# Routed attention and a SiLU MLP on one core: one-hot codes turned by themselves, new engine choices and a new order of heads

## The chip, the cores and the metric

The kernel runs on one core of a Trainium2 chip. The time is the device time of one execution in microseconds (us); the median of three runs of the kernel before is 308.21 (307.46 to 309.07). Lower is better. The engines are named as in the profile: PE (TensorE, its weight loads are PEld), DVE (VectorE), ACT (ScalarE), POOL (GpSimd), SP (SyncE, which here only issues transfers).

## The reference, cut to what matters

```python
# attention: q, k, v are (4, 8, 768, 64), centroids (8, 16, 64)
q_n = q / (np.linalg.norm(q, axis=-1, keepdims=True) + 1e-06)
k_n = ...
c_n = ...
q_assign = np.argmax(np.einsum('bhsd,hcd->bhsc', q_n, c_n), axis=-1)
k_assign = np.argmax(np.einsum('bhsd,hcd->bhsc', k_n, c_n), axis=-1)
mask = q_assign[:, :, :, None] == k_assign[:, :, None, :]
scores = np.where(mask, scale * np.matmul(q, k.transpose(0, 1, 3, 2)), -1000000000.0)
attn = softmax(scores)
attn_out = np.matmul(attn, v)
# MLP: x is (3072, 512), w_in (512, 2048), w_out (2048, 512)
x = attn_out.transpose(0, 2, 1, 3).reshape(B * S, H * D)
h = x @ w_in
return (h * (1.0 / (1.0 + np.exp(-h)))) @ w_out
```

Each query and each key is given to the nearest of 16 centroids of its head; a query attends only to the keys of its own centroid. The result of all heads goes through an MLP. `softmax` stands for the max, exp, sum and division of the source.

## The kernel before

**Scheme.** Tokens lie in tiles of 128, six tiles for a sequence (NJ = 6), so that a head's q and k are 12 tiles of 128 x 64. Each is multiplied by 128 and split into a high and a low half in fp16 (`hi`, lines 527 to 531, and `lo`, line 535), which lie side by side in a tile of `hl`, 128 columns. That tile is turned, so that features lie on partitions: by TensorE through a PSUM bank (line 570, copied out by a "settle", lines 585 and 587, into `lt`), which batch 0 does, or by one turning transfer of 12 tiles from `hl` into `ab` (line 550, issued by SP), which the other three batches do. The turned tiles are multiplied with the split centroids `stk` (lines 615 and 619 where the two terms add in the bank, `twin`, else line 624). From these logits VectorE takes the best centroid (a reduction and a comparison), which gives a code of 16 columns for every token, a mark at the query's centroid or at all but the key's. The code stands beside the high half in the scores product (line 801): 64 rows of data and 16 of code, so that a query and a key of other centroids get a term of 16384 in size that takes the exponential to 0. The exponential is on ScalarE (line 808), 288 of 128 x 512; the product with V (line 829) has a column of ones that yields the sum; VectorE takes the reciprocal (842) and normalises (847) into `xn`, one `xn` for the two heads of a pair. `xn` is turned into `xt`, by TensorE and a copy (877, 882, 884) or by a transfer (866). The MLP runs by units of two or three token tiles: up (907), tanh on ScalarE (913), gate on VectorE (918), down (942), copied out by ScalarE or VectorE (955, 957) and stored by SP (960). With y = h/2, SiLU is y(1 + tanh(y)).

**Codes before.** In batch 0 the code is written beside the high half in `hl`, and high half and code, 80 columns, are turned a second time by TensorE, one tile at a time (line 570 again, 96 tiles in all). The copy out of the bank multiplies each partition by `gain`, 1 for the data and 16384 for the code (lines 581 and 583), into `ab`. In the later batches VectorE turns the codes in blocks of 32 x 32 (line 715), and four copies put the quarters of a tile's tokens into rows 64 to 79 of `ab`: three on GpSimd (line 732), one as a transfer of SP (line 728), for each of the 24 heads.

**Loops.** Work is cut into parts (`part`): in batch 0 a head or a pair of heads with its keys and its first two query tiles, then the other four query tiles; later one head with 12 tiles. Batch 0 goes in two rounds, `ROUNDS` (0,2) and (2,6): all eight heads with two query tiles, then all eight with four; each of the others goes by heads over six tiles. MLP units lie between heads, as they become ready and by the due times `ML`.

**What sets the order.** Every operation is a `step` with an engine, a planned duration, what it comes after, the buffers it uses and a due time (`key`). A planner (class `Plan`) runs through time, gives each free engine its most urgent ready step, and the instructions are then emitted in the planned order; each engine executes its own in that order, and semaphores hold the real dependences. Buffers come from rings of fixed counts (`nk` and `nq` hold loaded K and Q, `nv` the loaded V, `hl`, `ab`, `vt` V in fp16, `P` exponentials, `Df` and `oh` and `ohT` stages of the codes, and eight PSUM banks); a step that needs a ring's next buffer waits until its old content has been read. Loads of K, Q and V, turning transfers and stores are all issued by SP in planned order; weights by GpSimd, each behind a tiny `pace` copy (line 974). Where the planner sees TensorE idle early in the run, it puts in "unread" matmuls of zeros (line 353, 128 x 256), as long as planned time is below `UNREAD`, 80000 ns.

**Choices.** The lists of lines 305 to 323 say which engine does what: `VC` casts V (line 415 on ACT, 417 on POOL), `TK` and `TQ` the settles of batch 0's first round, `TR` and `TS` of its second, `HI` and `HR` its high splits, `PUTB` the four code copies of the later batches, `XT` and the last argument of `attention` how `xn` is turned, `EVAC` the copies of the MLP's output. `AT` holds the due times of the rounds, `LEADS` how far ahead of them parts are started.

**Centroids.** They are loaded first, squared and summed, and their norm is taken as a power of 0.5 on GpSimd (line 433); then they are divided, split, turned by TensorE and put into `stk` by four copies.

## Time and profile before

| | before |
|---|---|
| median of 3 runs | 308.21 us (307.46 to 309.07) |
| the profiled execution | 307.14 us |
| its span in the trace | 305.3 us |
| mean granted TensorE clock | 0.998 |
| first unread matmul / first real instruction on TensorE | 1.05 / 5.53 us |
| first scores / first MLP matmul / first tanh | 11.82 / 34.90 / 35.96 us |
| end of the last matmul | 301.65 us |
| exponentials (L808, ScalarE) | 288, 157.8 us |
| down (L942), up (L907), scores (L801), V product (L829) on TensorE | 97.1, 95.6, 90.9, 49.8 us busy |
| code copies on GpSimd (L732) | 72, 39.3 us |
| code copies as transfers of SP (L728) | 24 |
| casts of V on GpSimd (L417) | 26, 14.6 us |
| lower splits on VectorE (L535) | 62, 40.7 us |
| tanh (L913), gates (L918) | 144 and 144, 67.8 and 70.1 us |

How to read it: the span runs from the first to the last instruction of the profiled execution, and the execution's own time has about 1.8 us around it. Busy times of TensorE overlap (a matmul starts before the one before it has ended), so that they add to more than the span holds; what one instruction costs is the time between its start and the next one's. The idle time of an engine is put down to the one that released it. An instruction's form reads output <- inputs, partitions x elements and type, so that "bank<-ident,hl 128x128" is a turn of a 128-column tile of `hl` into a PSUM bank, and "ab<-hl" a turning transfer.

### The profile page before, as it was taken

What the parts mean: (1) busy time and instruction counts of PE and PEld (TensorE: products, weight loads), DVE (VectorE), ACT (ScalarE), POOL (GpSimd) and SP (SyncE); (2) the same over time, 40 slices, a digit from 0 to 9 for tenths busy, and PEclk for the clock granted to TensorE, in tenths of its full rate; (3) what the DMA queues carried; (4) which work ended last, traced back from release to release, by engine and by line L of the source; (5) the groups of instructions that cost most, each with busy time, mean ns of one, the idle gap of its engine ahead of it and who ended that gap; (6) DMA issues with size and microseconds to landing.
All of it is one profiled execution on the core that took longest, in us unless ns stands there. A gap on an engine that the chain in (4) does not pass through costs nothing.

```text
span 305.3 us, 8425 instructions
## 1 busy us (share of the span) xinstructions
PE 297.3 (97%) x3257; PEld 196.1 (64%) x3257; DVE 207.9 (68%) x493; ACT 223.7 (73%) x461; POOL 108.2 (35%) x218
## 2 busy tenths in 40 slices
PE   8999999999999999999999998999999999999995
PEld 6898777577677746666656765665655565554644
DVE  5999688778869955989766997867562323750820
ACT  5869999888988838999777998778782380642721
POOL 2546432656466480717564563733000000000000
PEclk9999999999999999999999999999999999999999
DMA  7999969993969888486969848472010201002001
GB/s 245 290 249 251 206 104 224 103 248 87 226 100 237 191 167 196 138 156 162 237 149 223 155 154 169 131 129 66 0 37 36 84 12 71 35 0 73 32 34 69
DMA packets 73688, 41.82 MB, mean 137 GB/s; under 512 B 53041, under 2 KB 70705, under 8 KB 73649
## 3 DMA queue, kind: packets, MB, share of 16 engines
q1 hardware_dynamic: 68944, 36.94, 51.4%
q0 software_dynamic: 4288, 4.20, 8.6%
q8 instruction: 25, 0.41, 0.6%
q10 hardware_dynamic: 416, 0.16, 0.2%
q14 instruction: 15, 0.11, 0.1%
HBM read 27.30 MB, written 6.29 MB: 110 GB/s over the span
## 4 chain that ended last, share of the span: by engine, by line
PE 80%; DMA 7%; ACT 5%; DVE 3%; issue 1%; POOL 1%; SPq 0%; ACTq 0%; POOLq 0%
PE bank L942 27%; PE bank L907 22%; PE bank L801 16%; PE bank L829 9%; ACT P L808 4%; DMA ab<-hl 3%; PE bank L570 3%; DMA wout_s<-in_moe_w_out_dram 2%; PE bank L624 2%; DMA nk<-in_k_dram 2%; POOL hl L531 1%; PE bank L615 1%; DVE hl L535 1%; DVE gq L918 1%; PE bank L619 1%
## 5 line engine op out<-in xcount | busy, mean ns | idle before, releaser
L808 ACT ACTIVATE P<-bank 128x512 f16<-128x512 f32 x288 | 157.8, 640 | 30.8 <-PE bank L801 29.1
L942 PE MATMUL bank<-wout_s,gq 128*128 128x512 f16 (+1 forms) x400 | 97.1, 370 | 0.4 <-DMA wout_s<-in_moe_w_out_dram 0.4
L907 PE MATMUL bank<-xt,win_s 128*128 128x384 f16 (+1 forms) x576 | 95.6, 308 | 0.0
L918 DVE SCALAR_TENSOR_TENSOR gq<-tn,bank 128x384 f16<-128x384 f32 (+1 forms) x144 | 70.1, 504 | 32.4 <-ACT tn L913 28.7
L801 PE MATMUL bank<-ab 80*128 80x256 f16 (+1 forms) x384 | 90.9, 326 | 0.0
L913 ACT ACTIVATE tn<-bank 128x384 f32<-128x384 f32 (+1 forms) x144 | 67.8, 488 | 24.1 <-PE bank L907 20.9
L907 PEld LDWEIGHTS <-win_s 128*128 128x128 f16 x576 | 55.0, 97 | 28.8
L942 PEld LDWEIGHTS <-gq 128*128 128x128 f16 x400 | 37.9, 98 | 33.1 <-issue 0.7
L829 PEld LDWEIGHTS <-P 128*128 128x128 f16 x1152 | 45.6, 97 | 11.9 <-ACT P L808 0.8
L829 PE MATMUL bank<-vt,P 128*128 128x65 f16 x1152 | 49.8, 193 | 0.7 <-ACT P L808 0.6
L732 POOL COPY ab<-ohT 16x384 f16<-16x384 f16 x72 | 39.3, 546 | 28.2 <-DVE ohT L715 11.7
L801 PEld LDWEIGHTS <-ab 80*128 80x128 f16 x384 | 34.6, 97 | 20.7 <-DVE ab L583 0.2
L673 POOL TENSOR_TENSOR Df<-L,mx 128x192 f32<-128x192 f32 x24 | 12.3, 511 | 41.9 <-DVE mx L661 39.7
L957 DVE COPY ot<-bank 128x512 f32<-128x512 f32 x18 | 12.3, 681 | 16.4 <-PE bank L942 15.6
L535 DVE SCALAR_TENSOR_TENSOR hl<-nk,hl 128x384 f16<-128x384 f32 (+1 forms) x29 | 19.8, 687 | 3.3 <-POOL hl L531 3.1
L535 DVE SCALAR_TENSOR_TENSOR hl<-nq,hl 128x384 f16<-128x384 f32 (+3 forms) x33 | 20.9, 635 | 0.6 <-POOL hl L531 0.3
L641 DVE TENSOR_REDUCE L<-bank 128x192 f32<-128x384 f32 x24 | 13.3, 552 | 10.0 <-PE bank L624 9.7
L847 DVE TENSOR_TENSOR xn<-bank,rz 128x384 f16<-128x384 f32 (+2 forms) x40 | 19.1, 477 | 1.4 <-DVE rz L842 0.2
L531 POOL TENSOR_SCALAR hl<-nk 128x384 f16<-128x384 f32 (+1 forms) x25 | 13.6, 547 | 7.6 <-PE bank L570 6.7
L955 ACT COPY ot<-bank 128x512 f32<-128x512 f32 (+1 forms) x7 | 3.7, 524 | 17.2 <-PE bank L942 17.2
L531 POOL TENSOR_SCALAR hl<-nq 128x384 f16<-128x384 f32 (+2 forms) x27 | 15.2, 566 | 1.7 <-DMA nq<-in_q_dram 1.1
L417 POOL CAST vt<-nv 128x384 f16<-128x384 f32 x26 | 14.6, 582 | 1.1 <-DMA nv<-in_v_dram 0.7
(60 smaller groups left out, 183.6 us busy)
## 6 DMA issues: line engine op xcount, KB each, us to landing
nv<-in_v_dram SPq DMA_DIRECT2D x16, 384.0 KB, 5.6
out_dram<-ot SPq DMA_DIRECT2D x23, 256.0 KB, 2.3
nk<-in_k_dram SPq DMA_DIRECT2D x15, 384.0 KB, 4.3
nq<-in_q_dram SPq DMA_DIRECT2D x12, 384.0 KB, 4.7
wout_s<-in_moe_w_out_dram POOLq DMA_DIRECT2D x8, 256.0 KB, 7.2
win_s<-in_moe_w_in_dram POOLq DMA_DIRECT2D x4, 512.0 KB, 9.3
nq<-in_q_dram SPq DMA_DIRECT2D x4, 256.0 KB, 6.5
nk<-in_k_dram SPq DMA_DIRECT2D x2, 192.0 KB, 2.8
```

Source lines behind the costliest of these rows:

```text
L417: (nc.gpsimd if eng == "POOL" else nc.vector).tensor_copy(dst, src)
L531: nc.gpsimd.tensor_scalar(out=dh, in0=src, scalar1=qs, scalar2=1.0, op0=ALU.mult, op1=ALU.mult)
L535: nc.vector.scalar_tensor_tensor(out=dl, in0=src, scalar=qs, in1=dh, op0=ALU.mult, op1=ALU.subtract)
L732: nc.gpsimd.tensor_copy(dst, src)
L801: nc.tensor.matmul(banks[sb.i][:, at : at + 128 * (c1 - c0)], ab[0:80, kt[j], :], ab[0:80, qt + c0 : qt + c1, :].rearrange("p n c -> p (n ...
L808: nc.scalar.activation(out=T["P"][P.i][:, 0:at], in_=banks[sb.i][:, 0:at], func=AF.Exp, bias=0.0, scale=ESC if b else -ESC)
L829: nc.tensor.matmul(banks[O.i][:, (D + 1) * t : (D + 1) * t + nn], w, vt[:, VW * j : VW * j + nn], start=(j == 0), stop=(j == NJ - 1), skip ...
L847: nc.vector.tensor_tensor(out=T["xn"][xn.i][:, 0:nq, (h % 2) * D : (h % 2) * D + D], in0=banks[O.i][:, 0 : (D + 1) * nq].rearrange("p (t c ...
L907: nc.tensor.matmul(banks[bank.i][:, 0:n], win_s[:, r, ts(fb, 128)], T["xt"][xtb[b].i][:, r, 128 * j0 : 128 * j1], start=(r == 0), stop=(r ...
L913: nc.scalar.activation(out=T["tn"][tn.i][:, 0:n], in_=banks[bank.i][:, 0:n], func=AF.Tanh, bias=0.0, scale=1.0)
L918: nc.vector.scalar_tensor_tensor(out=T["gq"][g.i][:, fb % 4, 0:n], in0=T["tn"][tn.i][:, 0:n], scalar=1.0, in1=banks[bank.i][:, 0:n], op0=A ...
L942: nc.tensor.matmul(banks[bank.i][:, 0 : c1 - c0], T["gq"][gqs[fc // 4].i][:, fc % 4, ts(t, 128)], wout_s[:, fc, c0:c1], start=(fc == 0), s ...
```

## The change

All of the data's arithmetic stays; who does it, how the codes get into place, and the order differ.

- **Codes in batch 0.** The code now goes into a buffer of its own, `oh`, 32 columns for a tile. The turned tiles are settled straight into `ab` (`lt` is gone), and only the one-hots are turned: four tiles in one instruction of 128 columns, two in one of 64, or one in one of 32 (`TQ` and `TS` give the form). The 16 rows of each are then copied from the bank into `ab`'s rows 64 to 79, times ONE = 15360, on ScalarE (A), VectorE (D), or, by way of a copy `oc` of the whole bank, on GpSimd (P). `gain` is gone.
- **Codes of the later batches.** The fourth quarter goes by a copy on VectorE instead of the transfer of SP (`PUTB`).
- **Splits.** Batch 0's second-round high splits are on ScalarE; in two parts GpSimd does both halves (`LO` "P", function `both`, three instructions).
- **V.** Three casts of batch 0's four pairs on GpSimd, the fourth on VectorE; before, three on ScalarE and one on GpSimd.
- **Centroids.** Only the root stays on GpSimd and its key is made urgent; the turn makes both copies of the high half, so that one copy fills `stk`, which was four copies and a memset.
- **xn.** Batch 0's second round and the last head of each later batch are turned by transfers (`XT`, `XL`). Where two heads fit a bank (two query tiles), both are normalised by one reciprocal and one product.
- **MLP.** For units of two tiles two blocks of `w_in` share a bank, so that tanh and gate handle 512 columns at once.
- **Buffers.** `nk` 4 to 2, `nq` 5 to 3, `nv` 2 to 1, `ab` 5 to 3, `vt` 10 to 5, `gq` 7 to 5, `xt` 3 to 2, `L` 2 to 1; `P` 18 to 23, `xn` 3 to 13, `rz` 3 to 13, `Df` 2 to 9, `oh` 2 to 5, `ohT` 3 to 9, `tn` 3 to 4, `ot` 2 to 5; `oc` and `xs` with 4 each are new.
- **Order.** Due times are now given for each four heads (`wanted`) and a lead for each part, so that the planner takes heads 0 to 3 with all their queries, both rounds, before heads 4 to 7. In the planner several transfers at once share the engines with an exponent (`SHARE`), VectorE gets 110 ns for a step that follows its own, and unread matmuls end at 45000 ns of planned time.

```diff
-    UNREAD = 80000.0
+    UNREAD = 45000.0
-    MORE = 250.0
+    MORE = 0.0
-    AT = [32.0, 63.0, 104.0, 133.9, 193.2, 273.6]
-    ML = [55.5, 127.6, 75.5, 138.3, 182.4, 254.3, 222.5, 316.0, 335.3, 350.3]
-    PUTB = ["POOL", "POOL", "SP", "POOL"]
-    VC = ["ACT", "ACT", "POOL", "ACT"]
+    AT = [-892.1, 99.7, 38.0, -54.5, 191.8, 391.7, 459.8, 591.2, 689.2, 944.0, 1086.6]
+    ML = [-187.0, 482.9, 238.2, 499.0, 694.5, 447.4, 1168.0, 693.0, 1221.9, 1289.8]
+    PUTB = ["POOL", "POOL", "POOL", "DVE"]
+    VC = ["POOL", "POOL", "POOL", "DVE"]
     VB = "POOL"
-    TK = ["ACT", "ACT", "DVE", "DVE", "DVE"]
-    TQ = ["DVE", "ACT", "DVE", "DVE", "DVE"]
-    TS = ["ACT", "DVE", "DVE", "DVE"]
+    TK = ["ACT", "DVE", "ACT", "DVE", "DVE"]
+    TQ = ["DDPP", "DDDD", "2DA", "1DA", "2DD"]
+    TS = ["PDDP", "1DD", "1DA", "2DD"]
-    HR = ["DVE", "POOL", "DVE", "POOL"]
+    HR = ["ACT", "ACT", "ACT", "ACT"]
+    LO = ["P", "D", "D", "P"]
...
-    XT = ["DVE", "ACT", "ACT", "DVE"]
+    XT = ["ACT", "DVE", "DVE", "DVE", "DMA", "DMA", "DMA", "DMA"]
+    XL = ["DMA", "DMA", "DMA"]
...
     def c_place():
-        pt = banks[pc.i].bitcast(f16)
-        hi = pt[0:64, 0:128].rearrange("d (h c) -> d h c", c=HC)
-        nc.vector.tensor_copy(stk[0:64, :, 0:HC], hi)
-        nc.vector.tensor_copy(stk[64:128, :, 0:HC], hi)
...
+        nc.vector.tensor_copy(stk.rearrange("p s h c -> p (s h c)"), banks[pc.i].bitcast(f16)[:, 0 : 2 * H * HC])
...
+            def both(views=views, qs=qs, m=m):
+                src, dh, dl = views()
+                x = T["xs"][xs.i][:, 0 : 64 * m].rearrange("p (h j d) -> p h j d", h=src.shape[1], d=D)
+                nc.gpsimd.tensor_scalar(out=x, in0=src, scalar1=qs, scalar2=1.0, op0=ALU.mult, op1=ALU.mult)
+                nc.gpsimd.tensor_copy(dh, x)
+                nc.gpsimd.tensor_tensor(out=dl, in0=x, in1=dh, op=ALU.subtract)
...
-            for c in chunks:
-                bank = buf("M")
-                x = step("PE", 57 * len(c), turn_of(c, bank, D, HW), after=[marks, his, s_ident], use=[hl, bank], key=key + 12 * span)
...
+                def turn_code(c0=c0, c1=c1, bk=bk):
+                    for i in range(c0, c1, side):
+                        m = min(side, c1 - i)
+                        at = (i - c0) // side * 128
+                        nc.tensor.transpose(
+                            banks[bk.i].bitcast(f16)[0 : 32 * m, at : at + 128],
+                            T["oh"][oh.i][:, i : i + m, :].rearrange("p n c -> p (n c)"), ident,
+                        )
...
+                    def put_alone(c0=c0, c1=c1, bk=bk, on_a=on_a, cols=cols, g=g):
+                        dst = T["ab"][A.i][64 : 64 + HC, a0 + c0 + g : a0 + c1 : side, :]
+                        src = banks[bk.i].bitcast(f16)[32 * g : 32 * g + HC, 0:cols].rearrange("p (n c) -> p n c", c=128)
+                        if on_a:
+                            nc.scalar.activation(out=dst, in_=src, func=AF.Copy, bias=0.0, scale=ONE)
+                        else:
+                            nc.vector.tensor_scalar(out=dst, in0=src, scalar1=ONE, scalar2=None, op0=ALU.mult)
...
         n, h = divmod(place, H)
-        per = (AT[n + 1] - AT[n]) / H
+        per = wanted(place + 1) - wanted(place)
...
-            attention(n - NU + 1, h, 0, NJ, want[n, h], per, "DVE" if h == H - 1 else "DMA")
+            attention(n - NU + 1, h, 0, NJ, want[n, h], per, XL[n - NU] if h == H - 1 else "DMA")
```

In the changed kernel the lines that the prediction names are: L548 the lower splits (L535 before), L710 and L712 the code copies of the later batches on GpSimd and VectorE (L732 and L728).

## The prediction

> **What bounds the kernel now.** The page first, then the chain of waits in order of time, TensorE's timeline, and the waits by who waited for whom. Times are microseconds (us) unless marked ns.
>
> ```profile
> span 305.3 us, 8425 instructions
> ...
> PE 297.3 (97%) x3257; PEld 196.1 (64%) x3257; DVE 207.9 (68%) x493; ACT 223.7 (73%) x461; POOL 108.2 (35%) x218
> ...
> PE 80%; DMA 7%; ACT 5%; DVE 3%; issue 1%; POOL 1%; SPq 0%; ACTq 0%; POOLq 0%
> ```
>
> TensorE is busy for 97% of the span and is 80% of the chain that ended last. Busy includes matmuls that overlap in the array, so I cost one by the time from its start to the next one's. Chain of waits (start, length, what):
>
> ```profile
> 13.31 1.79 PE bank L570 x32
> ...
> 66.19 4.81 PE bank L907 x44
> ...
> 270.49 10.36 PE bank L942 x48
> 280.85 10.40 PE bank L907 x64
> ```
>
> A 128-wide turn takes 1.79/32 = 56 ns, 256 columns 4.81/44 = 109, 512 columns 10.36/48 = 216, 384 columns 10.40/64 = 162.
>
> ```profile
> 5.59 0.61 PE L570 MATMUL bank<-ident,hl 128*128 128x128 f16 x8
> 6.04 0.93 PE L353 MATMUL bank<-zeros 128*128 128x256 f16 x7
> 6.80 0.72 PE L570 MATMUL bank<-ident,hl 128*128 128x128 f16 x8
> ...
> 9.80 0.17 PE L615 MATMUL bank<-stk,lt 128*128 128x16 f16 x1
> 9.82 0.17 PE L619 MATMUL bank<-stk,lt 128*128 128x16 f16 x1
> 9.85 0.17 PE L615 MATMUL bank<-stk,lt 128*128 128x16 f16 x1
> ```
>
> In this timeline seven unread fillers (L353) take 6.80 - 6.04 = 0.76, 109 ns each, and a narrow logit 25 ns. With 30 ns for a 65-column product (12 in 0.36) the real work adds up: 368 + 192 of 512 columns, 384 of 384, 32 + 192 + 192 of 256, 1152 of 65, 223 turns and 480 logits make 121.0 + 62.4 + 45.3 + 34.6 + 12.5 + 12.0 = 287.8. The span is then: 5.5 until the first real instruction (28 fillers run there), 287.8 of work, 14 later fillers at 1.5, 3.7 after the last matmul (301.65), and a rest of 6.8 in which TensorE waits. Only fillers, turns, waits and the two ends can change. By the gaps between starts, some 4.1 of the waiting falls before 65 us (0.55 of it on a wout load at 53.6), 1.8 on three late turning transfers (103, 137 and 188 us), the rest in steps of 0.06.
>
> ```profile
> ACT P L808 <- PE bank L801: 29.1, 37, 10.3
> ...
> PEld L624 <- DMA ab<-hl: 3.5, 6, 1.2
> ...
> ACT vt L415 <- DMA nv<-in_v_dram: 2.2, 1, 2.2
> ```
>
> ScalarE waits for scores (late in the run, where it has slack). The six weight loads that wait for a turning transfer ab<-hl, and the 2.2 in which ScalarE stood before a V cast at 20 us, are what TensorE's own waiting hangs on.
>
> **The change, part by part.** I counted the changed kernel's instructions from its built order.
>
> Turns. Codes were turned with the 64 high rows, 96 turns of 80 rows; now the one-hots go alone: 6 turns of four tiles, 20 of two, 32 of one, 58. The centroids take 2 instead of 1. xn is turned on TensorE 8 times instead of 30 (four more transfers, and the last head of each later batch now goes by transfer). 223 becomes 164: 59 x 56 ns = -3.3. 41 of these lie before 65 us.
>
> Fillers. 64 instead of 42, 28 of them again before the first real instruction: 36 later ones against 14, 22 x 109 ns = +2.4. They are executed, so they cost this if TensorE has something to do there, and nothing if it would have waited.
>
> Start. First scores stand at 11.82 in the chain. The new chain by rows: k1's high half on ScalarE ends at 7.21 as now; behind it the second q split (0.4) and the copy of head 0's tiles (0.9) end at 8.5; logits at 8.6 to 9.4; VectorE's reductions and marks until 10.57; code turns, then six 256-column copies. No row has a 16-row, 256-column copy from PSUM: 128x256 xt<-bank (278 ns) is below, 128x512 hl<-nq (416) above; nearest in size is the first, 0.25 from start to start. Head 0's other two quarters go by a 0.2 copy and two GpSimd copies (between 0.42 and 0.55 each, L531 with 256 elements and L732 with 384) to 11.8. TensorE's ten fillers end at 11.95. So scores at 11.95, +0.15 (0 to +0.8), counted in the ramp's waits below.
>
> The ramp. The new order does heads 0 to 3 for all queries first, so that the first MLP matmul stands behind 56 exponentials, where it was behind 33. Groups of ScalarE from the first exponential to the first tanh, now:
>
> ```profile
> L808 ACT ACTIVATE P<-bank 128x512 f16<-128x512 f32 x33 | 17.2, 649 | 0.6 <-PE bank L801 0.6
> L581 ACT ACTIVATE ab<-bank,gain 80x1024 f16<-80x1024 f16 x2 | 2.3, 1143 | 0.0
> L415 ACT CAST vt<-nv 128x384 f16<-128x384 f32 x4 | 1.8, 509 | 2.2 <-DMA nv<-in_v_dram 2.2
> ```
>
> New: 56 x 0.48 (six in 3.02 less their overlap), two code copies at 1.0, a settle at 0.9, two 512-element splits at 0.5, an xt copy at 0.35: 31.2. The first exponential starts at 12.5 (a k split of 0.84 must precede it). I find 1.8 idle: 0.55 for the turns of head 2's codes, 0.65 because VectorE's half of these codes is made to wait for ScalarE's half in the same bank, and small ones. First tanh at 45.5; the scores of five exponentials ahead of it are already in banks (5 x 0.48), so TensorE starts the MLP at about 43.1. Work and fillers in front of it add to 41.3: 1.8 of waiting. Now the same sum is 32.3 and the trace has
>
> ```profile
> 34.90 1.37 PE L907 MATMUL bank<-xt,win_s 128*128 128x256 f16 x11
> ```
>
> 2.6. From there to 65 us the trace adds 1.5; after, I put 1.2, since the first turning transfers have 4 or more of TensorE's work between what they wait for and their reader, beyond a landing of 4.1 (their row of issues), except one with 2. Together 3.0 for 4.1: -1.1 (-2.5 to +4).
>
> Later turning transfers. In both orders I counted TensorE's work between the last thing that such an issue waits for and the first logit, less 4.1. Six of the 20 after 65 now have under 2.7 us, and two of the six are the waits of 0.54 and 1.10. In the new order four do. A third of 1.8: -0.6 (-1.8 to +4).
>
> VectorE's new copies. The last quarter of 24 code tiles went by SP and now goes by VectorE: 24 copies. On the other side it loses 11 wide settles (0.68 and 0.74) for 18 smaller code copies, 4 output copies, 24 gates by pairing, 4 recips and 4 norms by pairing, and four splits; with the new copies at 0.3 its 207.9 would fall by some 5. ScalarE gains as little by 24 paired tanhs and more output copies; neither is the bound after the ramp. No row has the copy: the 0.28 above is below it, and 0.28 + 0.55, one GpSimd copy, above. What VectorE does when GpSimd works can be seen:
>
> ```profile
> 121.01 0.20 DVE L700 TENSOR_SCALAR oh<-Df 128x96 f16<-128x96 f32 x1
> ...
> 124.73 0.51 DVE L702 TENSOR_SCALAR oh<-Df 128x96 f16<-128x96 f32 x1 [0.23 <-POOL Df L673]
> 125.15 0.56 DVE L700 TENSOR_SCALAR oh<-Df 128x96 f16<-128x96 f32 x1
> ```
>
> The same mark takes 0.20 with GpSimd idle and 0.51 to 0.56 beside its splits. The Trainium skill, page "SBUF — State Buffer", section "Who interferes with whom", says that VectorE's two-port copies and GpSimd share one port pair under an exclusive lock, and the later one blocks for the whole instruction; these rows agree, and by that rule the new copy, issued together with three GpSimd copies, often waits one out. I take 0.6 (nearer to the marks' row than to a free copy), 24 x 0.6 = 14, hidden as long as the lower splits behind it in VectorE's order (L548) still meet their transfer. If not, rival C.
>
> Casts of V and splits on GpSimd (30 casts for 26, two lower splits) are hidden: it is 35% busy. Fewer buffers (nk 4 to 2, nq 5 to 3, nv 2 to 1, ab 5 to 3) put waits into SP's queue: each V load waits for both casts of the one before, and behind it stand k, q and the turns. Hidden by the 20 us that two heads take, against a landing of 5.6; not in the ramp (rival D).
>
> End. The last head's xn was turned by TensorE with 28 down matmuls behind it as cover. Now it goes by transfer: rz 0.2, xn 0.56, waits 0.25, landing 3.6 (2.5 to 5.3) against 4.6 of work in between: +0.2 (0 to +1.7).
>
> Sum: -3.3 + 2.4 - 1.1 - 0.6 + 0.2 = -2.4. The profiled execution took 307.14 (its span and 1.8 around it): 304.7. The runs shown have the median 308.21, 0.35% above that execution; scaled so, 305.8. I say 305.3, between, and give the rivals on the median's scale.
>
> **Rivals.**
>
> A, the ramp does better: waits fall to the small steps. For it: ScalarE waits for no V cast any more, and 24 small code transfers leave SP. Against: 2.0 of waiting are already counted. If 3 more of the 6.8 go: 302.7.
>
> B, nothing: 41 of the 59 turns lie in the ramp, which ScalarE sets (14.74 of 15.00 busy from 30 to 45 us now). Then 2.3 of the 3.3 and the 2.4 of fillers are both mere waiting, and 18 x 56 ns, less the end's 0.2, are left, without the gains on waits: -0.8, 307.4.
>
> C, slower by VectorE: the new copy and its blocking push the lower splits, and with them ab<-hl. Today eight reads already wait for it; if each of these moves by one GpSimd copy (0.55), 4.4, and the -0.6 is gone: 304.7 + 5.0 = 309.7, or 310.8. It decides from the point where a split comes later than the 2.7 us of cover. For: the two long waits of today followed late splits. Against: VectorE's total falls.
>
> D, slower by SP's queue: a V buffer not free holds all loads behind it, and the fourth cast stands on VectorE in front of the codes. The one such wait now, 2.2 on ScalarE, cost TensorE 0.9. Four of them, with the ramp's -1.1 gone: 304.7 + 4.7 = 309.4, or 310.5. Against: by rows the fourth load lands 1 to 2 us ahead of its cast.
>
> The change does what it says: the counts above are from its own instructions.
>
> **How the numbers follow.** Forecast 0.42 (own range 303.5 to 306.6), A 0.13, B 0.19, C 0.14, D 0.12. About 0.5% is what a measurement here can tell from no change: 306.7 to 309.7. Faster 0.42 + 0.13, same 0.19, slower 0.26. The range 301.3 to 311.3 reaches past A and to C, and leaves out a ramp that fails altogether.
>
> **What would show it.** Right: 164 turns, first scores near 12, first MLP matmul at 43 to 44, first tanh near 45.5, waits before 65 near 3, no ab<-hl wait over 0.6, under 0.5 of waiting in front of the last batch's first MLP matmul. Wrong: a first MLP matmul after 46 (D, if SP or a cast stood before it), VectorE's L712 above 0.8 with ab<-hl waits above 5 in all (C), waits before 65 equal to the fillers saved (B).

## The result and the profile after

The changed kernel took 309.0 us (median of 20 runs), the kernel before beside it 307.45 (20 runs): a ratio of 1.0059, with a 95% interval of 1.0041 to 1.0078. It is 0.6% slower, where 305.3 us, a faster kernel, was forecast. A second measurement later gave 1.0048 (1.0024 to 1.0072). The profiled execution took 308.96, its span is 306.75. The ratios below leave out executions more than 1.5% above the fastest of the same kernel, which matters for `n4_few` alone (three of six, 316.78 to 318.77 us). The kernel before had medians from 307.44 to 308.12 us in the six measurements, so a difference of 0.2 or 0.3% between ratios of different measurements decides nothing.

Page of the changed kernel (span; busy time; shares of the chain that ended last):

```profile
span 306.8 us, 8227 instructions
...
PE 299.4 (98%) x3220; PEld 195.9 (64%) x3220; DVE 207.3 (68%) x483; ACT 222.0 (72%) x437; POOL 113.1 (37%) x223
...
PE 86%; POOL 4%; ACT 3%; DVE 3%; issue 2%; DMA 2%; POOLq 0%; ACTq 0%; DVEq 0%
```

TensorE is still the bound, and no other engine's total moved by more than 5 us (GpSimd 108.2 to 113.1, ScalarE 223.7 to 222.0). New is GpSimd with 4% of the chain (1% before). TensorE's waits behind 60 us say why (who waited for whom: total, times, longest):

```profile
PEld L848 <- POOL ab L710: 1.8, 2, 1.1
PEld L613 <- DMA ab<-hl: 1.3, 1, 1.3
```

Before, no scores (L801) waited for a code copy of GpSimd there. Now two do, and one turning transfer is late, where the prediction counted three.

I made the prediction's account again for two profiled executions of each kernel (the second ones are the runs `c_after` and `b_again` below). The unit costs are the prediction's but for the 65-column product: from start to start it takes 29 ns, not 30, which is 1.2 of the 1.5 us between the prediction's 287.8 of work and the 286.3 here. So the kernel before waits for 8.1 us in its first profile, not 6.8. Work is what TensorE's real instructions need, waits are what is left between their starts:

| term, us | forecast | measured |
|---|---|---|
| turns: work 286.3 to 283.0 | -3.3 | -3.3 |
| fillers behind the first real instruction, 3.9 against 1.5 | +2.4 | +2.4 |
| until the first real instruction, 6.99 and 6.64 against 5.53 and 6.44 | 0 | +0.8 |
| waits until 65 us, 4.8 and 5.0 against 4.3 and 3.0 | -1.1 | +1.3 |
| waits from 65 to 120 us, 3.2 and 3.2 against 0.7 and 0.8 | -0.6 with the next | +2.5 |
| waits behind 120 us, 1.4 and 1.4 against 3.1 and 3.1 | | -1.7 |
| behind the last matmul, 3.2 against 3.7 | +0.2 | -0.5 |
| sum (spans 306.75 and 306.54 against 305.34 and 305.14) | -2.4 | +1.4 |

Work left at a given time tells where the loss arises:

| TensorE work left, us, at | 13 | 35 | 48 | 65 | 120 | last matmul ends |
|---|---|---|---|---|---|---|
| before | 281.3 | 261.0 | 248.4 | 232.6 | 178.2 | 301.65 |
| before, second profile | 281.3 | 261.4 | 248.6 | 232.2 | 178.0 | 301.43 |
| changed | 279.6 | 262.1 | 250.3 | 233.7 | 181.8 | 303.56 |
| changed, second profile | 279.5 | 261.9 | 250.2 | 233.5 | 181.7 | 303.37 |

The changed kernel starts 3.3 ahead, by the turns it saved; at 13 us it is 1.7 ahead. By 48 us it is 1.8 behind, by 120 us 3.6. Some 1.7 comes back behind 120. Of the 3.5 lost between 13 and 48 us, its unread matmuls there take 1.7 (17 of them, where the kernel before has one); the rest is waiting.

One sentence of the section on the change has to be put right: as built, the order is not heads 0 to 3 with all queries and then 4 to 7. Two query tiles of heads 0 to 3 and 5 come first, then mixed the second rounds of 3, 2, 4 and 5 with the first rounds of 4, 7 and 6, then 6's second round. The second rounds of 7, 1 and 0 follow when the MLP has begun.

### The profile page after: what moved, and what is told of

It reads as the page before. It is cut to its first block, busy times and chain, and to the rows that moved or that the text cites. A ratio compares the mean times of both kernels' runs of the same rounds, so it can differ in the third digit from the quotient of the medians.

```text
span 306.8 us, 8227 instructions
## 1 busy us (share of the span) xinstructions
PE 299.4 (98%) x3220; PEld 195.9 (64%) x3220; DVE 207.3 (68%) x483; ACT 222.0 (72%) x437; POOL 113.1 (37%) x223
## 4 chain that ended last, share of the span: by engine, by line
PE 86%; POOL 4%; ACT 3%; DVE 3%; issue 2%; DMA 2%; POOLq 0%; ACTq 0%; DVEq 0%
PE bank L1000 26%; PE bank L966 25%; PE bank L848 18%; PE bank L879 9%; PE bank L360 3%; PE bank L613 2%; ACT P L855 2%; DMA ab<-hl 2%; POOL ab L710 2%; PE bank L734 1%; DVE hl L548 1%; PE bank L577 1%; POOL hl L537 1%; PE bank L608 0%; PE bank L604 0%
## 5 line engine op out<-in xcount | busy, mean ns | idle before, releaser
L855 ACT ACTIVATE P<-bank 128x512 f16<-128x512 f32 x288 | 151.8, 634 | 11.4 <-PE bank L848 10.0
L977 DVE SCALAR_TENSOR_TENSOR gq<-tn,bank 128x384 f16<-128x384 f32 (+1 forms) x120 | 68.1, 575 | 41.5 <-ACT tn L972 37.2
L972 ACT ACTIVATE tn<-bank 128x384 f32<-128x384 f32 (+1 forms) x120 | 62.9, 532 | 41.4 <-PE bank L966 40.8
L966 PE MATMUL bank<-xt,win_s 128*128 128x384 f16 (+1 forms) x576 | 92.6, 308 | 0.0
L848 PE MATMUL bank<-ab 80*128 80x256 f16 (+1 forms) x384 | 87.4, 325 | 1.6 <-POOL ab L710 1.0
L710 POOL COPY ab<-ohT 16x384 f16<-16x384 f16 x72 | 40.3, 559 | 31.2 <-DVE ohT L694 10.4
L1015 DVE COPY ot<-bank 128x512 f32<-128x512 f32 (+1 forms) x14 | 9.1, 648 | 20.1 <-PE bank L1000 20.1
L548 DVE SCALAR_TENSOR_TENSOR hl<-nk,hl 128x384 f16<-128x384 f32 (+1 forms) x29 | 20.8, 717 | 2.4 <-POOL hl L537 1.4
L424 POOL CAST vt<-nv 128x384 f16<-128x384 f32 x30 | 15.7, 532 | 17.4 <-DMA nv<-in_v_dram 8.9
L548 DVE SCALAR_TENSOR_TENSOR hl<-nq,hl 128x384 f16<-128x384 f32 (+3 forms) x31 | 19.5, 632 | 2.5 <-ACT hl L533 1.3
L905 DVE TENSOR_TENSOR xn<-bank,rz 128x384 f16<-128x384 f32 (+1 forms) x36 | 18.3, 508 | 0.7
L1013 ACT COPY ot<-bank 128x512 f32<-128x512 f32 x11 | 6.5, 594 | 12.7 <-PE bank L1000 12.7
L694 DVE STREAM_TRANSPOSE ohT<-oh 128x384 f16<-128x384 f16 x24 | 13.8, 574 | 0.5
```

What stands on the lines that cost most here:

```text
L424: (nc.gpsimd if eng == "POOL" else nc.vector).tensor_copy(dst, src)
L548: nc.vector.scalar_tensor_tensor(out=dl, in0=src, scalar=qs, in1=dh, op0=ALU.mult, op1=ALU.subtract)
L710: nc.gpsimd.tensor_copy(dst, src)
L848: nc.tensor.matmul(banks[sb.i][:, at : at + 128 * (c1 - c0)], ab[0:80, kt[j], :], ab[0:80, qt + c0 : qt + c1, :].rearrange("p n c -> p (n ...
L855: nc.scalar.activation(out=T["P"][P.i][:, 0:at], in_=banks[sb.i][:, 0:at], func=AF.Exp, bias=0.0, scale=ESC if b else -ESC)
L905: nc.vector.tensor_tensor(out=dst, in0=sums()[:, :, 0:D], in1=T["rz"][rz.i][:, 0:n].unsqueeze(2).to_broadcast([128, n, D]), op=ALU.mult,)
```

## Experiments

Most edits keep the planned order and change only what is issued (lines stay those of the changed kernel). Ratios are to the kernel before, measured beside the run, with 95% intervals.

### The first 48 us: fillers, K loads, exponentials

`e1_fill` leaves out the 36 later fillers:

```diff
-    for s in plan.order():
-        s.fn()
+    order = plan.order(); zero = [s for s in order if s.key == 1e9][28:]
+    [s.fn() for s in order if s not in zero]
```

> The changed kernel without its 36 unread matmuls behind the first 28; every other instruction and its order stays. Theory R (ScalarE sets the time of the first 48 us, so whatever TensorE does there beside it is free): the first MLP matmul stays at 47.2 +- 0.4, the time stays at the changed kernel's 1.006 of the kernel before (+- 0.002), and TensorE's waits before 65 us grow by the 3.9 us of the fillers. Theory F (fillers cost what they take, as the prediction had it): first MLP matmul near 44, time 2 to 4 us less, 0.993 to 1.0. Should the array drop to half rate without them, narrow turns at 107 instead of 56 ns would show it, and the time would rise.

Measured: 1.0095 (1.0059 to 1.0131), 311.12 us, where `e2_kbuf` and `e3_wlate` beside it, which keep the fillers, took 309.27 and 308.72. So it is slower without them. First the changed kernel's window from 13 to 30 us, then two of this run (us; busy time of PE, PEld, DVE, ACT, POOL with instruction counts; granted TensorE clock, DMA share, GB/s):

```profile
13.00:30.00 17.00, 16.30 (x275) 13.21 (x274) 11.35 (x27) 15.98 (x29) 7.90 (x16) 1.00 0.94 201
```

```profile
13.00:30.00 17.00, 15.53 (x230) 12.59 (x228) 9.61 (x23) 13.39 (x24) 6.75 (x13) 0.76 0.83 175
30.00:48.00 18.00, 17.54 (x302) 12.77 (x302) 12.81 (x37) 16.73 (x35) 10.58 (x19) 1.00 0.99 192
```

The granted clock was 0.76 between 13 and 30 us (0.50 from 11 to 21), and by 48 us 252.9 of work were left, 2.6 more than with fillers. So neither theory holds: the fillers are not free padding, and not a pure cost of 3.9. Without them six of eight executions had a mean granted clock of 0.994 or less, with them 5 of 32 (the changed kernel). The fall itself is not theirs alone: `e2_kbuf` and `d1_two`, with fillers, show it at 11 us too, but for 3 us. Nor is the clock all: the two executions at 0.999 and 1.000 took 309.38 and 310.26, so leaving the fillers out gains nothing even there.

`e2_kbuf` gives K of the third and fourth pair memory of their own; `e3_wlate` issues the first weight transfer with the second:

```diff
-            e.dma_start(T["nk"][x.i][:, hs[0] : hs[-1] + 1, :], rows(k, b, h0, h1, 0, NJ))
+            e.dma_start(knat(b, p, x)[:, hs[0] : hs[-1] + 1, :], rows(k, b, h0, h1, 0, NJ))
...
+            late.append((kind, n))
+            for kd, m in late[:2] if len(late) == 2 else late[-1:] if len(late) > 2 else []:
...
```

> The changed kernel with K of batch 0's third and fourth pair loaded into memory of their own (two gate tiles, idle until 47 us), so that SP's queue does not stop for a K buffer at 4 us; order on every engine as it is. Theory R: these loads are issued at 3.6 and 4.1 instead of 6.57 and 8.70, ScalarE's split of 768 elements no longer stands in front of the first exponential until 13.73, which comes at 12.6 to 13; first MLP matmul 0.7 to 1.2 us earlier (46.0 to 46.5), time 1.002 to 1.004. Theory S (the loss is TensorE's half rate until 7.0 us in the profiled execution, nothing else): no change, 1.006. If the earlier loads only slow the first pair's by contention: second split at 7.2 instead of 6.84, and 1.006 to 1.008.

> The changed kernel with the first weight transfer (512 KB of w_in, issued at 4.53) issued with the second one at 14.9. Theory R: the K split of the second pair on ScalarE starts near 6.4 instead of 6.84, K of the third pair lands 1 to 2 us earlier, first exponential at 12.6 to 13.2 instead of 13.73, time 1.003 to 1.005. Theory S: no change, 1.006. If w_in comes too late for the first MLP matmul, that moves past 48 and a wait on w_in is seen in front of it.

Measured: 1.0045 (1.0019 to 1.0071) and 1.0044 (1.0015 to 1.0072). Against the changed kernel's 1.0059 and 1.0048 that is no difference that these runs can tell. The loads did come earlier in `e3_wlate` (first exponential 12.66 instead of 13.73, first MLP matmul near 46.8), and it bought next to nothing. The profiled execution of `e2_kbuf` ran at half rate from 11 to 14 us, so that its start can't be read.

`x1_exp` halves 49 of batch 0's exponentials (from a P tile's second use on):

```diff
-                nc.scalar.activation(
+                at = at // 2 if b == 0 and P.i in full else full.add(P.i) or at; nc.scalar.activation(
```

> The changed kernel with 49 of batch 0's 72 exponentials on half of their columns (256 instead of 512), 33 of them in front of the first MLP matmul; the other halves of these tiles are left out, so the attention of batch 0 is not computed. Theory R (ScalarE's 56 exponentials set the first 47 us): ScalarE has 33 x 0.21 = 7 us less before the first tanh, TensorE's own work becomes the bound there (7.0 + 35.9 = 43), first MLP matmul at 42.5 to 44.5 instead of 47.2, time 2.5 to 4 us less than the changed kernel: 0.992 to 0.998. If TensorE or VectorE sets the ramp: first MLP matmul within 1 us of 47.2, 1.003 to 1.006.

Measured: 1.0075 (1.0045 to 1.0105), first MLP matmul at 46.7. The same window of the changed kernel and of this one:

```profile
30.00:48.00 18.00, 17.88 (x312) 13.18 (x309) 13.87 (x39) 16.64 (x34) 11.22 (x19) 1.00 1.04 217
```

```profile
30.00:48.00 18.00, 18.00 (x314) 13.85 (x311) 14.29 (x40) 11.05 (x36) 11.66 (x19) 1.00 1.11 231
```

ScalarE (fourth pair) lost 5.6 of its 16.6 busy, TensorE (first pair) was busy nearly all the time in both, and got through some 0.4 more of its work. Theory R falls for 30 to 48 us: with TensorE's order as it is, ScalarE does not set the time there. Between 13 and 30 us, where ScalarE was as busy as before (15.98), this run says nothing. The time did not fall either, since the scores of batch 1 then waited 2.3 for one of GpSimd's code copies, at 66 to 68 us.

### The code copies of the later batches

`e4_sp4` issues the fourth copy on SP in the place of VectorE's copy, `e5_sp4p` tells the planner too, `d1_two` gives VectorE two of the four:

```diff
-                def put(g=g):
+                def put(g=g, code_eng=["POOL", "POOL", "POOL", "SP"]):
...
-    PUTB = ["POOL", "POOL", "POOL", "DVE"]
+    PUTB = ["POOL", "POOL", "POOL", "SP"]
...
+    PUTB = ["POOL", "POOL", "DVE", "DVE"]
```

> The changed kernel with the fourth quarter of the later batches' codes on a transfer of SP again, as in the kernel before, instead of VectorE's 24 copies; order otherwise as it is. Rival C of the prediction (these copies and their blocking delay the lower splits and so the turning transfers): 1 to 4 us less, 0.995 to 1.003, and the wait of 1.2 at 114 us shrinks. Theory R: nothing beyond 0.5 us, 1.004 to 1.008, since the copies took 0.26 to 0.45 each; the waits at 67 and 72 us, which are on GpSimd's copies, stay.

> The changed kernel with the fourth quarter of the later codes on SP's transfer again, this time told to the planner, so that it places the transfers (the run with the transfer in the copy's place came out at 1.0485). Theory O: 1.006 to 1.015, first MLP matmul unmoved at 46 to 48, since the copies on VectorE cost next to nothing and the transfers stand in SP's queue. Rival C of the prediction: 0.995 to 1.003.

> The changed kernel with two of the four code copies of the later batches on VectorE and two on GpSimd (one and three before), known to the planner. Theory G (GpSimd's copies come late where heads follow each other closely, as at 67 and 72 us, and VectorE's cost little): the waits of the scores on GpSimd's copies fall from 2.8 to under 1.5, time 0.3 to 1.5 us less than the unchanged one beside it. Theory V (rival C of the prediction: copies on VectorE delay the lower splits and so the turning transfers): waits on turning transfers rise over 3 us, time 0.5 to 2 us more.

Measured: 1.0485 (1.0444 to 1.0527), 1.0011 (0.9989 to 1.0033) and 1.0045 (1.0017 to 1.0073). The first is some 13 us slower than the changed kernel: TensorE waited 11.4 us between 75 and 120, mostly in front of scores. In the longest of these waits, 4.4 us at 81, the codes were ready (L694) at 78.45, but the transfer was issued only at 80.97, behind a turning transfer in SP's queue, and landed at 84.94. Behind that wait the granted clock was 0.50 from 86 to 88 us. With the planner told, which then places everything anew, the same transfers cost nothing, and the kernel is as fast as the one before, within the interval; TensorE's waits from 65 to 120 us are 1.1 instead of 3.2. Taken alone that speaks for rival C; `o4_sp` below, where the same exchange made another schedule 1% slower, speaks against it. With two copies on VectorE the time is the same: the waits of scores from 65 to 120 us fell from 1.5 to 0.6, and those on turning transfers rose from 1.2 to 1.8. Theories G and V each have half of it.

`x2_copies` leaves out GpSimd's 72 code copies:

```diff
                     elif code_eng[g] == "POOL":
-                        nc.gpsimd.tensor_copy(dst, src)
+                        pass
```

> The changed kernel with GpSimd's 72 code copies of the later batches left out (the scores read old codes there). Theory G (after 60 us codes come with no lead, and each delay on GpSimd is TensorE's wait): the waits at 67 and 72 us go, 1.4 us, and with 40 us less on GpSimd VectorE's splits are not slowed, so that the wait of 1.2 at 114 shrinks as well: time 1 to 2.5 us less than the changed kernel, 0.997 to 1.002. If these waits only move to the turning transfers: 1.003 to 1.006, with waits on turning transfers above 2.

Measured: 0.9985 (0.9959 to 1.0011), so 0.6 to 0.7% below the changed kernel, some 2 us. No scores waited for codes; the turning transfer at 112 us still came 1.3 late. The span fell to 305.2, by 1.6. Theory G holds, with one reserve: 40 us of GpSimd's work that can slow VectorE's splits went with the copies. How the wait at 67 us came about is seen in GpSimd's and VectorE's timelines of the changed kernel (start, length, what):

```profile
64.51 1.04 POOL L710 COPY ab<-ohT 16x384 f16<-16x384 f16 x2 [1.13 <-issue]
65.63 0.70 POOL L537 TENSOR_SCALAR hl<-nq 128x384 f16<-128x384 f32 x1
66.39 0.89 POOL L710 COPY ab<-ohT 16x384 f16<-16x384 f16 x1
```

```profile
63.83 0.56 DVE L694 STREAM_TRANSPOSE ohT<-oh 128x384 f16<-128x384 f16 x1
...
65.15 0.81 DVE L548 SCALAR_TENSOR_TENSOR hl<-nk,hl 128x384 f16<-128x384 f32 x1
...
66.36 0.56 DVE L548 SCALAR_TENSOR_TENSOR hl<-nq,hl 128x384 f16<-128x384 f32 x1
```

The codes are ready (L694) at 64.39. Three copies and a high split stand in GpSimd's queue; split and last copy take 0.70 and 0.89 instead of 0.50 beside VectorE's lower splits, and the scores can go at 67.34. TensorE stood from 66.68.

That such a delay shows at all is a matter of lead. The time from the end of a head's last code copy on GpSimd or VectorE to its first scores, for the first six heads of batch 1: 2.4, 8.2, 5.8, 6.8, 8.0 and 8.3 us before; 0.3, 0.1, 0.1, 0.4, 1.4 and 0.7 in the changed kernel. Before, the fourth copy was a transfer; with its landing counted too, the leads before are 1.5, 6.4, 3.8, 6.7, 3.9 and 8.3.

### Order, buffers and due times

`o1_old` and `o2_old` put the old order of heads back, with all new instructions and more buffers; `o3_new` is a schedule of the changed order with other due times and the changed kernel's buffers for loads. The planner's lists alone differ (two of them, `o1_old` here):

```diff
-    COUNT = [2, 3, 1, 3, 3, 5, 23, 5, 2, 13, 1, 2, 9, 5, 9, 4, 5, 13, 4, 4]
+    COUNT = [3, 4, 2, 3, 4, 13, 19, 10, 2, 3, 1, 1, 6, 2, 2, 2, 3, 1, 5, 2]
...
-    AT = [-892.1, 99.7, 38.0, -54.5, 191.8, 391.7, 459.8, 591.2, 689.2, 944.0, 1086.6]
+    AT = [-1110.5, -277.0, -200.0, -53.0, 174.4, 334.0, 381.8, 479.4, 612.9, 857.3, 1060.4]
...
```

> The changed kernel with all of its new instructions (code turns, copies, casts, paired tanhs), but with the order of the kernel before in the first 60 us: all eight heads with two query tiles, then all eight with four, the first MLP unit beside the second round. For that it has more buffers (ab 4, nk 3, nq 4, nv 2, vt 13; fewer xn, rz, Df, ohT) and other due times. Theory O (the order, which too few ab and K buffers force, leaves TensorE without MLP work until 47 us while 56 exponentials run on ScalarE): first MLP matmul at 34 to 37, TensorE's useful work done by 48 us 36 to 38 us instead of 32.7, time 0.985 to 0.998 of the kernel before. Theory P (the new instructions themselves cost: narrow turns, copies in VectorE's queue, transfers): first MLP matmul as early, but time 1.003 or more.

> As the run before, by another set of buffers (ab 5, xt 3, P 16) and due times, so that a lucky schedule is not taken for the order. Theory O: first MLP matmul at 35 to 38, time 0.985 to 0.998. Theory P: 1.003 or more.

> The changed kernel with its own order of heads (MLP behind some 57 exponentials; ab 3, nk 2, nq 3, nv 1 kept) and other due times, drawn in the same way as those of the two runs before. Theory O: first MLP matmul at 47 to 50, time 0.999 to 1.008. If instead it comes near the two before (below 0.998), it was the due times and not the order.

Measured: 1.0027 (1.0003 to 1.0051), 1.0011 (0.9987 to 1.0034) and 1.0072 (1.0045 to 1.0100); first MLP matmul at 36.4, 37.4 and 48.7. Theory O has the direction, but not the size: less than the 0.6% came back, though the MLP began 10 us earlier, and the interval of `o1_old` overlaps those of the changed kernel. By 48 us both old orders had caught up with the kernel before (248.0 and 247.7 of work left); by 120 us they had lost it again (181.0 and 179.4). In `o1_old` TensorE waited 3.8 us between 65 and 120, mostly in front of scores.

`o4_sp` and `o5_two` are `o1_old` with the fourth copy on SP, and with two copies on VectorE:

> The run with the old order (1.0027) and the fourth code copy on SP's transfer instead of VectorE, known to the planner: the new things that are left are the code turns, splits, casts and paired tanhs of batch 0. Theory V: the waits of the scores after 65 us (5.8 us in that run's trace) fall, 0.990 to 0.999. Theory G: they stay, and SP's queue adds its own, 1.002 to 1.010.

> The run with the old order (1.0027) and two code copies each on VectorE and GpSimd. Theory G: the waits of the scores after 65 us fall by a third or more, 0.994 to 1.001. Theory V: they stay or grow, and waits on turning transfers come on top, 1.003 to 1.010.

Measured: 1.0128 (1.0083 to 1.0172) and 1.0058 (1.0026 to 1.0089). Neither helps. Taken together, which engine makes a copy seems to count less than when it comes.

So the next schedules were drawn for lead, with more buffers, the old order of heads, and some other engine choices (V's casts, some high splits and turns of `xn`):

> All new instructions of the change, the old order of heads, more buffers (ab 4, nk 3, nq 4, nv 2, hl 4, vt 10, gq 9), V's casts on ScalarE twice, VectorE and GpSimd, and due times drawn for lead: codes and transfers planned so that later ones than planned do little harm. Theory O and G together (the order, and the lead that codes have on their scores): first MLP matmul at 39 to 41, codes 2 us or more ahead of their scores for the first six heads of batch 1, time 0.982 to 0.996. If it stays at 1.001 or more, lead and order are not what the change lost.

> As the run before, from another draw (ab 4, nk 3, nq 5, nv 2, xt 3; xn of batch 0 turned by TensorE, one lower split more on VectorE). The same expectations: 0.982 to 0.996 if order and lead were lost, 1.001 or more if not.

Measured: 0.9981 (0.9959 to 1.0002) and 1.0131 (1.0096 to 1.0167). `n1_new` has all of the change's new kinds of instructions and takes 307.18 beside 307.44: 0.7 to 0.8% below the changed kernel, level with the one before, and between the two forecasts. Its codes lead by 0.5, 0.1, 5.4, 7.0, 2.7 and 4.1 us, so two heads fall short of the 2 us asked for. `n2_new` lost 2.8 us at once, at 42 us, in front of a code turn, and behind that wait the granted clock was 0.50 from 46 to 48 us. Timelines of VectorE and GpSimd there (start, length, what):

```profile
39.58 3.48 DVE L548 SCALAR_TENSOR_TENSOR hl<-nk,hl 128x384 f16<-128x384 f32 x1
42.98 0.85 DVE L548 SCALAR_TENSOR_TENSOR hl<-nq,hl 128x384 f16<-128x384 f32 x1
```

```profile
39.37 0.52 POOL L537 TENSOR_SCALAR hl<-nk 128x384 f16<-128x384 f32 x1
39.83 0.95 POOL L424 CAST vt<-nv 128x384 f16<-128x384 f32 x2
40.75 0.51 POOL L537 TENSOR_SCALAR hl<-nq 128x384 f16<-128x384 f32 x1
41.22 0.50 POOL L537 TENSOR_SCALAR hl<-nk 128x384 f16<-128x384 f32 x1
41.70 0.50 POOL L537 TENSOR_SCALAR hl<-nq 128x384 f16<-128x384 f32 x1
42.15 1.27 POOL L424 CAST vt<-nv 128x384 f16<-128x384 f32 x2
```

One lower split took 3.48 instead of 0.55, while GpSimd ran eight splits and casts without a gap and at their usual pace but for the last; the marks of the waiting turn stood behind it. The two schedules, drawn alike, came out 1.5% apart.

`n4_few` takes buffers from `n1_new` and changes no other list; the planner then places the steps anew:

```diff
-    COUNT = [3, 4, 2, 4, 4, 10, 14, 9, 2, 3, 5, 8, 1, 2, 2, 5, 3, 3, 1, 4]
+    COUNT = [2, 3, 1, 3, 3, 10, 14, 9, 2, 3, 5, 8, 1, 2, 2, 5, 3, 3, 1, 4]
```

> The run n1_new (0.998) with the changed kernel's buffer counts for what is loaded and turned: nk 3 to 2, nq 4 to 3, nv 2 to 1, ab 4 to 3, hl 4 to 3; instructions, engine choices and due times stay, so the planner may only place steps later. Theory L (the change lost the preparation ahead, because too few buffers hold loads and turned tiles): VectorE idles more between 13 and 35 us (busy under 17 us there, where n1_new has 18.9), more planned gaps with unread matmuls, first MLP matmul 3 us or more later (44 to 48 instead of 41), time 1.004 to 1.015. If buffers are not the point but only due times and engine choices: 0.997 to 1.001.

Measured: 1.0163 (1.0094 to 1.0231), first MLP matmul at 48.1 instead of 40.8. What the engines did between 13 and 35 us (columns as above): the kernel before, the changed one, `n1_new` and `n4_few`.

```profile
13.00:35.00 22.00, 21.25 (x401) 18.54 (x400) 20.66 (x58) 19.45 (x39) 11.27 (x23) 1.00 1.12 248
```

```profile
13.00:35.00 22.00, 21.30 (x361) 16.57 (x360) 14.70 (x35) 20.98 (x39) 11.51 (x21) 1.00 0.95 189
```

```profile
13.00:35.00 22.00, 21.54 (x390) 17.84 (x388) 18.93 (x53) 20.26 (x39) 15.59 (x27) 1.00 1.00 209
```

```profile
13.00:35.00 22.00, 21.04 (x350) 16.74 (x349) 15.38 (x39) 17.70 (x35) 14.00 (x24) 1.00 0.85 191
```

Read the third pair, VectorE: 20.66 and 18.93 in the two faster kernels, 14.70 and 15.38 in the two slower ones. In this stage VectorE prepares the next heads (lower splits, settles, reductions, codes). K's buffers are 2 instead of 3, Q's 3 instead of 4, V's 1 instead of 2, `hl` and `ab` 3 instead of 4, and the loads go out later. The four V loads of batch 0 are issued at 3.7, 6.8, 10.3 and 15.2 us in the kernel before, at 3.7, 6.4, 12.7 and 17.8 in `n1_new`, but at 3.1, 9.6, 17.4 and 32.0 in the changed kernel and at 3.1, 10.0, 25.6 and 33.2 in `n4_few`. The longest wait of SP's queue from 13 to 35 us, before and in the changed kernel (total, times, longest):

```profile
SPq L404 <- ACT vt L415: 3.4, 1, 3.4
```

```profile
SPq L411 <- POOL vt L424: 11.0, 1, 11.0
```

A V load stood for 11.0 us behind GpSimd's cast of the V before it, and the first K of batch 1 behind that load. That VectorE idles because inputs are missing is argued from this; its own waits there end on ScalarE and TensorE. What it did not do then has to be done later, between GpSimd's copies and in front of TensorE's scores.

Theory L holds: on this schedule the buffers are worth 1.8% (by the intervals 1.1 to 2.5). The order goes with them. `n1_new` does all 48 narrow score products of batch 0's first round before the second round, `n4_few` 36 of them, and the rest in the midst of the second. VectorE's share goes by the buffers and not by due times or engine choices: with more of them for K, Q, V and `ab` it is busy in this window for 18.93, 19.15 and 18.50 us in `o1_old`, `o2_old` and `n2_new`, with the changed kernel's for 14.48 in `o3_new`. But that share alone does not give the time, as `n2_new` with its wait at 42 us shows. TensorE itself looks equally busy in all four rows (21.0 to 21.5), since fillers count as busy; of its work it does 20.3, 17.5, 18.8 and 16.0 us there.

### The same kernels again

> The changed kernel again, unchanged, on the same chip as the three runs beside it, as their measure: the theories agree on 1.004 to 1.008. Its profile shows how much the start differs from one execution to the next: half rate of TensorE until 4 to 7 us, first exponential between 12.5 and 14.7.

Measured: 1.0048 (1.0024 to 1.0072); first exponential 13.57, first MLP matmul 47.07, and the same waits at 67 (0.80), 72 (0.55) and 113 us (1.22).

> The kernel before once more, for a second profile of it. If the moment at which TensorE reaches full rate is a matter of the execution and not of the kernel, it differs from the 4.0 us of the first profile (4 to 7), first scores then come up to 1 us later than 11.82, and the span is 305.5 to 307. If it belongs to the kernel: 4.0 again and a span within 0.3 of 305.3.

Measured: 306.95, span 305.14. Its TensorE timeline:

```profile
1.05 5.55 PE L353 MATMUL bank<-zeros 128*128 128x256 f16 x28 [1.05 <-DVE zeros L331]
6.44 0.22 PE L446 MATMUL bank<-ident,chl 128*128 128x128 f16 x1
```

Full rate came at 5.9 us instead of 4.0, the first real instruction at 6.44 instead of 5.53, and yet first scores at 11.87 and the span stayed. So a later start of this size belongs to the execution, and the kernel before absorbs it ahead of its scores. The +0.8 of the account's third row is therefore not put down to the change.

## Why the prediction was wrong, point by point

- **Turns, -3.3:** right as counted and as timed: 164, and 3.3 us less work. 44 of the 58 code turns take 55 or 56 ns from start to start; four take 66 or 67, and behind the others TensorE waits.
- **Fillers, +2.4:** right in size, wrong in kind. The prediction took them to cost this or nothing; without them the kernel is slower still, in part by the clock.
- **Start:** scores forecast at 11.95, measured 12.62 and 12.46, within the bounds given; the second pair's K split ended at 7.68 instead of the assumed 7.21.
- **The ramp, waits 3.0 until 65 us instead of 4.1:** the first step that failed, and the largest: of the 3.8 us between forecast and measurement 2.4 arise here. The waits are 4.8 and 5.0, where the kernel before has 4.3 and 3.0. First MLP matmul 47.2 and tanh 48.6 where 43.1 and 45.5 stood, beyond the mark of 46 that the prediction set for being wrong. It costed the ramp on ScalarE, exponential by exponential, took VectorE's preparation as given, and put the fewer buffers at nothing there ("not in the ramp"). `x1_exp` shows that ScalarE does not decide behind 30 us; `n1_new` against `n4_few` that buffers for what is loaded and turned can decide the ramp. In the changed kernel itself this is not shown: the one run that gives it buffers back, K's in `e2_kbuf` with the order as it was, gained nothing.
- **Late turning transfers, -0.6:** right in the first profiles. 1.8 became 1.2, one wait, from a lower split that ended at 109.26 and a transfer landing 5.4 later. One wait is over 0.6, against the forecast's sign.
- **GpSimd "hidden: it is 35% busy":** the second step that failed. Two waits of TensorE, 0.82 and 0.55, hang on its code copies between 66 and 73 us, and leaving the copies out is worth about 2 us. The added casts and splits are not shown to be at fault. Between 60 and 75 us GpSimd is busy for 11.38 of 15 us, where it was 8.55, since five more instructions fall there (a copy, two high splits, a cast, a weight issue). But that share is no sure sign: in `n1_new` it is 11.72, and no scores wait for a copy by more than 0.3. What the sum had no term for is the lead of the codes on their scores.
- **VectorE's new copies at 0.6:** too dear. They took 0.34 on average, 8.3 in all, and VectorE's total fell by 0.6 instead of 5.
- **End, +0.2:** no wait for the last head's transfer was seen (0.05 behind 250 us); the tail got 0.5 shorter.
- **Rivals:** on the rivals' scale, where the kernel before has 308.21, the time is 309.8, between B on one side and D and C on the other. C's place was right in part: one of the waits is its (109 us); but the codes themselves were late, which no rival had. D has its sign, a first MLP matmul after 46, and its mechanism, a V load that holds the queue (11.0 us of waiting in SP). It priced that by ScalarE's wait for a V cast, though, and what it cost TensorE is not measured. B's idea that ScalarE covers the ramp falls with `x1_exp` for its second half.

Open: what sets 13 to 30 us in the changed kernel, where ScalarE is busy for 15.98 of 17 us; how much of the 0.6% is due times, order and buffers in the changed kernel itself, since its due times were made for few buffers and the order of heads followed the buffers in every run; whether `n1_new` owes part of its gain to its V casts, two of which are on ScalarE again; and why the fourth copy on SP's queue helps one schedule and hurts another. No kernel here is shown to beat the one before: `n1_new` is level with it.

## What to carry to other kernels

Cost a stage by what has to be ready at its end, and look for the lead: how long before its use each input is done. A kernel whose inputs lie microseconds ahead swallows a slower copy; one at 0.1 us can turn any contention into a wait of the bounding engine, though the engines' totals have hardly grown. And before buffers are taken from loads for other rings, see in the busy time by stage which engine works ahead there, and on what.

## What was not expected of the hardware

- **Half rate at the start is a matter of the execution.** The first 256-column fillers take 213 ns each, then 109; the change came between 3.8 and 6.9 us in the profiles of these runs, for the same instructions. The granted clock in the rows reads 1.00 in that time. The Trainium skill, page "TensorE: Matmul & The Clock Gate", section "Part 1: The HAM clock gate", says that the gate opens after a busy window of some 3.4 us that runs free of the kernel's start; the spread of 3.1 us agrees with that. The section also puts the spread at 500 ns either way, and these profiles do not agree with that.
- **The clock can fall again in the ramp, and behind a wait.** The profiled `e2_kbuf` ran at half rate from 11 to 14 us, after a stage in which TensorE was busy for two thirds:

```profile
8.00:11.00 3.00, 2.02 (x50) 1.85 (x51) 3.00 (x11) 1.80 (x3) 0.94 (x2) 1.00 1.16 290
11.00:14.00 3.00, 3.00 (x18) 2.20 (x18) 2.82 (x10) 1.98 (x3) 0.79 (x2) 0.50 1.13 308
```

  Executions with a mean granted clock of 0.993 or 0.994 were 5 of 32 of the changed kernel (310.05 to 310.95, the others' median 308.80), and 3 of 118 of the kernel before. Ten profiles have the changed kernel's start. In three of them (`e1_fill`, `e2_kbuf`, `d1_two`) the first filler at full rate starts by 4.2 us, and these three show the fall at 11 us; in the other seven it starts at 4.6 or later, and none does. Why is not shown. Two later falls stand behind long waits of TensorE (2.8 us in `n2_new`, 4.4 in `e4_sp4`), so that such a wait can cost more than its length; behind one of 2.5 at 231 us in `e4_sp4` there is none.
- **VectorE can stand for microseconds while GpSimd works.** A code copy takes 0.50 alone and up to 0.89 beside a lower split, a lower split 0.55 alone and up to 0.87 beside GpSimd: mostly both lose a little. In `n2_new` one lower split took 2.9 us longer during GpSimd's unbroken row (above), and one of `n1_new` took 2.23 during another, where the same form takes 0.87 at most in the changed kernel. That GpSimd is the cause is read from the overlap alone. The Trainium skill, page "SBUF — State Buffer", section "Who interferes with whom", has a VectorE instruction with two SBUF inputs, like the lower split, contend with GpSimd's reads, and in VectorE's two-port modes one engine blocked for a whole instruction of the other; here it was a row of them.
